# Another order of the same work, and other engines for part of it, in an attention-then-MoE kernel on one core

## The chip, the core and the metric

The kernel runs on one core of a Trainium2 chip. The metric is device time in microseconds from one execution; the median of several executions is given. The engines are TensorE (PE; its weight loads are shown as PEld), VectorE (DVE), ScalarE (ACT), GpSimd (POOL) and SyncE (SP). SP and GpSimd also issue most of the DMAs.

## The reference

```python
scores = scale * np.matmul(q, k.transpose(0, 1, 3, 2))     # q, k, v: 8 x 12 x 448 x 64, fp32
attn = np.maximum(scores, 0.0) ** 2 / S
attn_out = np.matmul(attn, v)
x = attn_out.transpose(0, 2, 1, 3).reshape(B * S, H * D)   # 3584 x 768
h = x @ w_in                                               # 768 x 2048
g = h * (1.0 / (1.0 + np.exp(-1.702 * h)))
out = g @ w_out                                            # 2048 x 768
```

## The kernel before

Attention is cut into 24 units of four heads each (8 batches, 3 units a batch). A unit's q and k are loaded, cast to fp16 and transposed. Then come seven `scores` words s (index j, 64 keys of each head at a time; four 64x64 matmuls of 448 columns into two PSUM banks), relus r out of PSUM to fp16 (one for each bank, on ScalarE or VectorE), one square x on each pair of relus in SBUF, and one `attn_v` word a of 28 matmuls, which needs all seven squares. Copies e bring its result to the token tiles xe and xo.

The token matrix is cut into eight groups g of 384 and 512 tokens in turn. The input product of group 0, and half of group 1, is done by plain matmuls (f, three words for one output tile, each two matmuls). The rest is done by a seven-product scheme in place of eight: sums S of w_in and T of the tokens on VectorE, seven products u of six matmuls, a snapshot t of a bank (ScalarE or VectorE), adds b on VectorE. A gelu g on ScalarE writes fp32 to a `gf` tile, and a widening v takes this to fp16 with a factor. The output product does the same: sums W of w_out and A of the gelus on VectorE, seven products p of eight matmuls for a pair of token tiles (or a single product i), snapshots h, last parts l (all but one kind only on VectorE), and stores o and q.

No scheduler orders this. The body holds one list of 1950 words, and each word issues its instructions when it is reached, under a manual schedule. `f0.2.1` is an f of group 0. `@4.5` names PSUM banks. `:d`, `:a` and `:p` put a word on VectorE, ScalarE or GpSimd, where it has a choice; without it the table `home` decides (`v` on GpSimd, `r`, `t`, `h` and `K` on ScalarE, `Q` on GpSimd) or VectorE takes it. Each engine executes its own instructions strictly in the order in which the words stand. An engine that waits, therefore, holds up all that stands behind it in its queue, DMA issues included. The places of words of different engines relative to each other mean nothing beyond the dependencies.

Loads are words too. On SP's queue: `Lk`, `Lq` load a unit's k or q as fp32 (then `K`, `Q` cast it on an engine, and `Rk`, `Rq` transpose it by DMA), the stores, and one gate `G3`, which waits for a part of w_in. On GpSimd's queue, in this order among its computing: `jk`, `jq` load and cast units 1 to 5, `V` the v of each unit, `jwa` and `jwb` the halves of w_in's four parts, `jo` the four quarters of w_out. Units 0 to 5 are transposed on TensorE (`tk`, `tq`, and copies `ek`, `eq`). `z` words are matmuls of zeros at the start.

The buffers that matter: 11 `at` tiles of squares, 5 `gf`, 3 `osb`, 3 each of `kT` and `qT`, 4 `v16`, one `kst` and one `qst`, and the eight PSUM banks.

```python
        home = {"K": "a", "Q": "p", "r": "a", "t": "a", "h": "a", "v": "p"}
```

```python
    def widen(e, o, i):
        eng[e].tensor_scalar(out=o, in0=i, scalar1=SC, scalar2=1.0, op0=ALU.mult, op1=ALU.mult)
```

In the profile, relus are at lines 161 (VectorE) and 163 (ScalarE), ScalarE's squares at 169, widenings at 217, sums, adds and VectorE's squares at 88, copies at 83, `scores` at 150, `attn_v` at 181, f at 228, all other products at 203, gelus at 214, v, q and k loads of GpSimd at 104, w_in at 411, w_out at 415.

Of the kernel before, what the change touches and what calls it, by code (L numbers as in the profile page):

```python
# [15 lines left out]
def kernel(  # L16
# [406 lines left out]
    with tc.manual_schedule():  # L423
# [35 lines left out]
        def zeros(e, p, n):  # L459
# [8 lines left out]
            "jq1 z13@0 Lk0 I K0:d tk0@1 ek0 z1 Lq0 Q0:a tq0@2 tq1@3 jk1 eq0 s0.1@4.5 jwb2 jk2 "  # L468
            "s0.6@6.7 s0.4@0.1 r0.4.0:d r0.6.0 tk1@2 ek1 jq2 jq3 eq1 s0.3@6.0 r0.1.1 r0.4.1 "
            "r0.1.0 x0.1 s0.0@5.2 r0.0.0 s0.2@1.4 r0.2.0:d r0.3.1:d r0.3.0 s0.5@3.5 r0.6.1 "  # L470
            "s1.1@6.1 r0.2.1 r0.0.1:d s1.2@7.0 s1.5@4.2 x0.0 r0.5.0 r1.1.1 r1.2.1 jk3 x0.4 "
            "r0.5.1:d tq2@3 r1.2.0 x0.2 x0.6:a x0.5 x0.3 V0 r1.5.1 s1.0@1.0 x1.2 tk2@7 r1.5.0:d "
            "r1.0.0 ek2 tk3@5 r1.0.1 jwa0 s1.3@2.1 eq2 r1.1.0 x1.1:a V2 a0@0.6 V1 x1.5:a r1.3.1 "
            "s1.4@4.7 ek3 r1.3.0 jq4 jwb0 s2.1@3.5 r1.4.1 e0.0.1 s2.2@1.2 r1.4.0:d jk4 e0.0.0 "
            "jwa2 s1.6@4.7 x1.3 r1.6.1:d r2.1.0 r2.2.1 tq3@3 r2.2.0 e0.1.0 x1.4 r1.6.0 x1.6 "
            "r2.1.1 x1.0:p s2.6@2.1 jwa1 x2.2 s2.0@7.0 r2.0.1 r2.0.0 a1@4.5 r2.6.1 jwb1 e0.1.1:a "
            "e1.0.0:a s2.5@0.7 s2.3@1.6 r2.3.0 r2.3.1 e1.1.0:a x2.1 eq3 r2.6.0:d e1.0.1:a "
            "s2.4@3.2 r2.5.0:d r2.4.0:d r2.4.1:d jk5 f0.3.0@1 r2.5.1:d f0.2.0@0 x2.0:p tq4@6 eq4 "
            "tk4@4 s3.3@3.2 x2.6:p x2.3:a e1.1.1:a x2.4:p s3.2@7.5 x2.5:a jq5 r3.2.1:d r3.3.1:d "
            "r3.3.0 r3.2.0 f0.3.1 V3 ek4 f0.2.1 f0.0.0@6 s3.0@5.3 a2@2.7 e2.0.0 r3.0.0 S2.1 "  # L480
            "r3.0.1 x3.0:a e2.0.1:a s3.1@4.5 r3.1.0 f0.1.0@3 f0.0.1 f0.1.1 f0.1.2 e2.1.0:a g0.1 "
            "f0.0.2 V4 V5 jwb3 f0.2.2 x3.2 jwa3 g0.0 r3.1.1:d g0.2 f0.3.2 g0.3 x3.3 e2.1.1 "
            "s3.4@4.2 s3.5@5.3 r3.4.1:d s3.6@6.7 f0.8.0@0 f0.8.1 f0.4.0@1 G3 v0.1 r3.5.1:d r3.5.0 "
            "r3.4.0 x3.4 x3.5 x3.1 f0.8.2 f0.4.1 f0.4.2 r3.6.1 g0.8 s4.1@2.5 r3.6.0 v0.3 r4.1.1:d "
            "s4.3@3.4 r4.1.0 s4.2@7.0 r4.2.1 g0.4 f0.6.0@6 f0.6.1 f0.6.2 r4.2.0:d x3.6 tq5@2 "
            "tk5@5 r4.3.0 r4.3.1 x4.3 g0.6 x4.2:a x4.1 ek5 s4.0@0.7 a3@1.3 r4.0.1 r4.0.0 v0.0 "
            "s4.6@4.6 s4.4@7.5 jo0.0 eq5 f0.10.0@0 r4.4.0:d f0.10.1 f0.10.2 x4.0 v0.8 e3.0.0:a "
            "r4.6.1:d r4.4.1 f0.7.0@2 s5.4@1.7 e3.0.1:a s4.5@5.3 r4.6.0 g0.10 s5.1@4.6 v0.10 "
            "r4.5.0 f0.5.0@0 f0.5.1 f0.5.2 x4.6 f0.11.0@5 f0.11.1 f0.11.2 v0.6 f0.7.1 r4.5.1 "
            "r5.4.1 r5.1.0:d r5.1.1:d g0.5 x4.5:a v0.5 f0.7.2 r5.4.0:d s5.0@4.3 x4.4 s5.2@7.6 "  # L490
            "a4@0.1 r5.0.0:d r5.0.1:d g0.7 g0.11 jo0.1 v0.11 s5.6@2.5 r5.2.1 r5.2.0 s5.5@4.6 "
            "s5.3@3.7 r5.6.0:d e4.0.1:a f0.9.0@1 r5.3.1:d r5.3.0 r5.5.1:d v0.7 S0.1 r5.6.1:d "
            "f0.15.0@2 f0.15.1 r5.5.0 f0.14.0@3 x5.6 f1.1.0@7 jo1.1 f0.14.1 x5.5 v0.4 x5.1:a "
            "f0.9.1 v0.2 S3.1 jo1.0 f0.9.2 g0.9 v0.9 f0.13.0@4 f0.13.1 f0.12.0@6 f0.12.1 f1.3.0@5 "
            "e4.0.0:a S2.2 x5.4 Lq6 f0.15.2 Lk6 x5.0:a x5.3:a S2.3 S1.1 x5.2 f1.7.0@1 f0.14.2 "
            "g0.14 f0.12.2 g0.15 g0.12 S3.2 f1.7.1 f0.13.2 f1.5.0@0 Q6:d f1.0.0@3 f1.1.1 S2.4 "
            "g0.13 v0.13 a5@2.6 v0.15 e5.0.0 K6 e5.0.1:a Lk7 v0.14 S1.2 f1.0.1 f1.5.1 T1.1 "
            "f1.4.0@4 T1.2 v0.12 f1.7.2 S3.3 T1.4 W2.1 W0.1 f1.5.2 g1.7 v1.7 f1.6.0@2 A0.0.1@0 "
            "Lq8 g1.5 W3.1 f1.4.1 f1.4.2 g1.4 W2.2 f1.0.2 g1.0 Rk6 Rq6 v1.5 v1.0 f1.6.1 f1.3.1 "
            "u1.2.0@6 f1.2.0@1 t1.2.0 f1.1.2 W1.1 f1.3.2 K7 Rk7 u1.3.0@0 u1.2.1@4 g1.3 g1.1 v1.1 "  # L500
            "v1.3 Q8:a v1.4 f1.6.2 f1.2.1 f1.2.2 g1.2 v1.2 p0.0.0@3 h0.0.0 V8 b1.2.1 t1.3.0:d "
            "u1.3.2 u1.2.2 u1.2.3 Lk8 V6 W2.4 W0.2 T1.3 W2.3 g1.2.1 g1.6 t1.2.2 K8:p s6.0@5.7 "
            "s6.2@1.2 v1.2.1 r6.0.0 W1.2 u1.2.4 W3.2 r6.2.1:d r6.0.1 r6.2.0 t1.2.4 x6.0:a W3.3 "
            "u1.3.1@5 p0.0.1@2 W3.4 b1.3.1 A0.0.2@1 Lq7 s6.1@7.1 u1.2.5 b1.2.3 r6.1.1 r6.1.0:d "
            "l0.0.1 u1.3.3 u1.2.6 s6.3@1.7 W0.4 x6.1:a p0.0.2 W1.3 b1.2.6 Rq8 g1.2.3 r6.3.0:d "
            "t1.3.2 s6.5@4.1 A0.0.4 h0.0.2:d r6.3.1 u1.3.4 W0.3 v1.2.3 p0.0.3 Q7:a v1.6 r6.5.0 "
            "s6.6@7.4 Lq9 Q9 r6.5.1 g1.3.1 g1.2.5 t1.3.4 x6.2:a S3.4 A0.0.3 x6.5:a r6.6.0 W1.4 "
            "v1.3.1 b1.3.3 x6.3 V7 s6.4@1.6 r6.4.0 p0.0.4 u1.3.6 h0.0.4:d u1.3.5 Rq7 r6.6.1 "
            "l0.0.3 r6.4.1:d b1.3.6 p0.0.5 g1.2.6 g1.3.5 s7.4@7.1 s7.0@4.6 g1.3.6 g1.3.3 v1.3.3 "
            "l0.0.5:a v1.3.6 x6.6 s7.2@5.0 r7.2.0 Lk9 x6.4 r7.4.1:d r7.4.0 p0.0.6 r7.2.1 r7.0.0:d "  # L510
            "Rk8 K9:p r7.0.1:d l0.0.6 v1.2.6 x7.0:a s7.1@3.1 r7.1.1 r7.1.0:d a6@5.4 e6.0.0 "
            "e6.0.1:a e6.1.1 Lk11 e6.1.0 s7.5@7.6 s7.3@0.2 r7.5.1:d p1.0.0@3 A0.2.5@1 r7.5.0 x7.1 "
            "r7.3.0 s8.0@1.4 x7.4 s7.6@5.7 r7.6.1:d r8.0.0:d s8.1@0.6 v1.2.5 v1.3.5 r7.3.1 x7.3:a "
            "i0.2.0@2 K11:p r8.1.1 r7.6.0 x7.2 Lq10 x7.5:a x7.6 S1.3 r8.0.1 S0.3 s8.2@6.7 "
            "r8.2.0:d r8.1.0 a7@5.1 s8.3@4.0 o0.1 e7.0.1 Rk9 Rq9 x8.1 r8.3.0:d x8.0 n0.2.0:a "
            "Q10:a r8.2.1 e7.1.1 A1.0.1@0 s8.6@2.6 x8.2:a r8.3.1 i0.2.1@7 r8.6.0 r8.6.1 x8.3:a "
            "h1.0.0 V11 s8.5@0.4 e7.0.0 r8.5.0 x8.6 s8.4@2.1 r8.4.0 r8.4.1 A1.0.2@1 r8.5.1:d "
            "p1.0.1@6 n0.2.1:a x8.4 p1.0.2 e7.1.0:a Lk10 s9.0@0.2 s9.1@1.4 r9.0.0:d r9.1.1:d "
            "l1.0.1 x8.5:a r9.0.1 r9.1.0 a8@7.5 s9.3@2.0 S1.4 x9.0 r9.3.0:d e8.0.0:a K10:p "
            "e8.0.1:a A1.0.4 T2.1 s9.2@1.4 p1.0.3 Rq10 S0.2 r9.2.1 h1.0.2 r9.2.0 r9.3.1 e8.1.0:a "  # L520
            "e8.1.1:a u2.1.0@4 u2.0.0@2 t2.0.0 t2.1.0 u2.0.1@1 s9.4@0.7 u2.1.1@5 Lq11 T2.2 r9.4.0 "
            "b2.0.1 x9.3 u2.1.2 u2.0.2 u2.2.0@0 T2.4 Q11:a b2.1.1 T2.3 g2.0.1 A1.0.3 u2.0.3 "
            "t2.0.2 Rk11 u2.0.4 t2.0.4:d o0.0 g2.1.1 t2.1.2 Rk10 b2.0.3 Lq12 r9.4.1 v2.1.1 u2.1.3 "
            "u2.1.4 Lk12 u2.0.5 t2.2.0 u2.2.1@7 S0.4 v2.0.1 u2.0.6 t2.1.4 x9.1:a b2.1.3 u2.1.6 "
            "b2.2.1 g2.0.3 g2.2.1 u2.2.2 v2.2.1 v2.0.3 b2.0.6 g2.0.6 g2.0.5 v2.0.6 b2.1.6 g2.1.3 "
            "Rq11 u2.1.5 t2.2.2:d v2.1.3 g2.1.5 v2.1.5 u2.2.3 u2.3.0@1 g2.1.6 u2.3.1@5 u2.2.4 "
            "v2.0.5 s9.5@2.4 t2.3.0:d b2.3.1 v2.1.6 u2.3.2 V9 t2.2.4 o0.2 b2.2.3 Q12:a t2.3.2 "
            "A1.2.1@0 A1.2.2@1 g2.3.1 u2.2.5 v2.3.1 u2.3.3 g2.2.3 u2.2.6 r9.5.1 u2.3.4 p1.0.4 "
            "t2.3.4:d u2.3.5 r9.5.0:d b2.2.6 g2.2.5 K12 Lq14 h1.0.4 Lk13 v2.2.3 g2.2.6 g2.3.5 "
            "s10.1@4.0 x9.2 r10.1.1 A1.2.3 x9.4:a l1.0.3 s9.6@2.7 p1.0.5 b2.3.3 s10.0@1.0 u2.3.6 "  # L530
            "v2.2.6 r9.6.0:d r9.6.1 r10.0.0 r10.1.0:d Rk12 V13 b2.3.6 x9.6:a r10.0.1:d Rq12 "
            "p1.2.0@2 g2.3.6 l1.0.5:a x9.5 p1.0.6 l1.0.6 h1.2.0 s10.3@7.4 g2.3.3 s10.2@1.5 Q14 "
            "r10.2.1 r10.2.0 r10.3.0:d a9@0.3 s10.6@6.5 s10.4@7.1 r10.6.0:d x10.0:a r10.6.1:d "
            "p1.2.2 r10.4.1:d e9.0.0:a e9.0.1 x10.1:a v2.3.5 h1.2.2 o1.1 p1.2.1@6 x10.2:a x10.6 "
            "s10.5@0.5 l1.2.1 s11.1@1.3 r10.3.1 r10.5.0:d r10.4.0 x10.4:a x10.3:a r11.1.0:d "
            "p1.2.4 r10.5.1:d r11.1.1:d p1.2.3 s11.0@4.7 s11.3@0.1 v2.2.5 x10.5 h1.2.4 r11.0.0:d "
            "V10 v2.3.6 a10@5.3 r11.3.1 r11.3.0 s11.2@4.1 e10.0.1:a r11.0.1:d l1.2.3 A1.2.4 "
            "v2.3.3 e10.0.0:a Lq13 Q13 K13:p s11.6@7.0 r11.6.0 p1.2.5 x11.1:a o1.0 r11.6.1:d "
            "r11.2.1:d r11.2.0 p1.2.6 A2.0.1@0 s11.5@3.5 s12.3@0.7 x11.0:a s11.4@1.4 l1.2.5:d "
# [135 lines left out]
```

## Time and profile before

| what | value |
|---|---|
| median of 3 runs | 369.36 us (368.82 to 371.6) |
| span of the profiled execution | 372.2 us |
| TensorE busy | 358.6 us, 96% of the span |
| VectorE busy | 302.9 us, 81% |
| ScalarE busy | 281.3 us, 76% |
| GpSimd busy | 137.6 us, 37% |
| granted TensorE clock, mean | 0.987 |
| HBM read, written | 45.61 MB, 11.01 MB |

The profile is of one execution, and its own time is its span, 372.2 us; what lies around the span is not recorded. It is above the slowest of the three timed runs. Busy time counts the union of an engine's instructions. Instructions of one engine overlap by some 0.1 us, so a row's mean duration times its count is more than the engine's busy time. A wait is put down to what ended it.

### The profile page before, as it was taken

What the parts mean: (1) busy time and instruction counts of PE and PEld (TensorE: products, weight loads), DVE (VectorE), ACT (ScalarE), POOL (GpSimd) and SP (SyncE); (2) the same over time, 40 slices, a digit from 0 to 9 for tenths busy, and PEclk for the clock granted to TensorE, in tenths of its full rate; (3) what the DMA queues carried; (4) which work ended last, traced back from release to release, by engine and by line L of the source; (5) the groups of instructions that cost most, each with busy time, mean ns of one, the idle gap of its engine ahead of it and who ended that gap; (6) DMA issues with size and microseconds to landing.
All of it is one profiled execution on the core that took longest, in us unless ns stands there. A gap on an engine that the chain in (4) does not pass through costs nothing.

```text
span 372.2 us, 9025 instructions
## 1 busy us (share of the span) xinstructions
PE 358.6 (96%) x3562; PEld 233.2 (63%) x3562; DVE 302.9 (81%) x556; ACT 281.3 (76%) x540; POOL 137.6 (37%) x202
## 2 busy tenths in 40 slices
PE   7699999799999999999999999999999999999994
PEld 4345554465559755786558755686559755688562
DVE  3988995899988989877998889898897899856552
ACT  3979985579989998798897898868887889346210
POOL 5859264714412732054411613344602421034300
PEclk9989999899999999999999999999999999999998
DMA  9999999918997791849965695784583242300334
GB/s 192 183 204 163 213 209 226 218 18 173 200 225 165 151 221 25 167 105 174 179 170 98 146 184 172 188 171 119 82 205 23 41 97 26 85 2 2 85 97 117
DMA packets 65226, 51.38 MB, mean 138 GB/s; under 512 B 35744, under 2 KB 61856, under 8 KB 65184
## 3 DMA queue, kind: packets, MB, share of 16 engines
q1 hardware_dynamic: 48176, 36.22, 43.2%
q0 software_dynamic: 16608, 14.09, 26.4%
q8 instruction: 28, 0.46, 0.5%
q10 hardware_dynamic: 400, 0.49, 0.4%
q14 instruction: 14, 0.11, 0.1%
HBM read 45.61 MB, written 11.01 MB: 152 GB/s over the span
## 4 chain that ended last, share of the span: by engine, by line
PE 84%; DMA 7%; DVE 3%; POOL 2%; ACT 1%; issue 1%; SPq 0%; DVEq 0%; ACTq 0%
PE ox L203 30%; PE hx L203 27%; PE sc L150 9%; PE av L181 8%; PE os L203 6%; DMA wout<-in_moe_w_out_dram 4%; PE ht L228 3%; DMA v<-in_v_dram 2%; DMA qst<-in_q_dram 1%; DVE wT L88 1%; PE tr L131 1%; POOL ge L217 1%; DVE at L88 1%; ACT gf L214 1%; POOL go L217 0%
## 5 line engine op out<-in xcount | busy, mean ns | idle before, releaser
L163 ACT ACTIVATE at<-sc 128x448 f16<-128x448 f32 x201 | 99.6, 559 | 13.0 <-PE sc L150 12.7
L161 DVE TENSOR_SCALAR at<-sc 128x448 f16<-128x448 f32 x135 | 79.8, 618 | 10.9 <-PE sc L150 10.6
L217 POOL TENSOR_SCALAR go<-gf 128x512 f16<-128x512 f32 x64 | 42.6, 665 | 79.1 <-ACT gf L214 75.7
L169 ACT ACTIVATE at<-at 128x896 f16<-128x896 f16 x72 | 68.2, 962 | 1.7 <-DVE at L161 1.2
L217 POOL TENSOR_SCALAR ge<-gf 128x384 f16<-128x384 f32 x64 | 35.4, 554 | 74.0 <-ACT gf L214 70.8
L203 PEld LDWEIGHTS <-win 128*128 128x128 f16 x624 | 56.7, 98 | 8.5 <-issue 2.4
L88 DVE TENSOR_TENSOR at<-at 128x896 f16<-128x896 f16 x92 | 55.9, 631 | 1.7 <-ACT at L163 0.6
L88 DVE TENSOR_TENSOR gf<-hx,gf 128x512 f32<-128x512 f32 (+1 forms) x78 | 47.7, 625 | 11.5 <-ACT gf L79 5.4
L150 PE MATMUL sc<-qT,kT 64*64 64x448 f16 x672 | 52.6, 363 | 1.3 <-DVE qT L83 0.6
L214 ACT ACTIVATE gf<-gf 128x512 f32<-128x512 f32 (+1 forms) x78 | 43.8, 585 | 11.7 <-DVE gf L88 11.6
L203 PEld LDWEIGHTS <-winS 128*128 128x128 f16 x468 | 43.4, 99 | 8.2 <-issue 3.9
L203 PE MATMUL ox<-wout,go 128*128 128x384 f16 x256 | 46.4, 326 | 0.0
L203 PEld LDWEIGHTS <-go 128*128 128x128 f16 x320 | 29.9, 98 | 23.2 <-issue 5.8
L203 PE MATMUL hx<-T,winS 128*128 128x256 f16 (+1 forms) x312 | 38.2, 268 | 2.7 <-DVE gf L83 2.7
L181 PE MATMUL av<-at,v 64*64 64x448 f16 x672 | 37.5, 357 | 1.0 <-DMA v<-in_v_dram 1.0
L203 PEld LDWEIGHTS <-ge 128*128 128x128 f16 x256 | 24.0, 98 | 18.4 <-issue 4.1
L150 PEld LDWEIGHTS <-kT 64*64 64x64 f16 x672 | 18.7, 106 | 26.3 <-issue 22.1
L79 ACT ACTIVATE gf<-hx 128x384 f32<-128x384 f32 (+1 forms) x44 | 23.3, 537 | 15.4 <-PE hx L203 12.0
L203 PE MATMUL ox<-wT,asum 128*128 128x384 f16 x192 | 34.9, 327 | 0.0
L203 PE MATMUL hx<-xo,win 128*128 128x256 f16 x252 | 31.4, 273 | 0.4 <-ACT gf L79 0.4
L203 PEld LDWEIGHTS <-asum 128*128 128x128 f16 x224 | 21.1, 98 | 16.3 <-issue 3.3
L81 ACT ACTIVATE osb<-ox 128x384 f32<-128x384 f32 x32 | 15.4, 496 | 19.2 <-PE ox L203 19.1
(75 smaller groups left out, 475.9 us busy)
## 6 DMA issues: line engine op xcount, KB each, us to landing
out_dram<-osb SPq DMA_DIRECT2D x52, 192.0 KB, 3.2
kst<-in_k_dram SPq DMA_DIRECT2D x19, 448.0 KB, 4.7
qst<-in_q_dram SPq DMA_DIRECT2D x19, 448.0 KB, 4.9
v<-in_v_dram POOLq DMA_DIRECT2D x24, 224.0 KB, 5.6
win<-in_moe_w_in_dram POOLq DMA_DIRECT2D x8, 384.0 KB, 9.7
wout<-in_moe_w_out_dram POOLq DMA_DIRECT2D x4, 768.0 KB, 11.5
q<-in_q_dram POOLq DMA_DIRECT2D x5, 224.0 KB, 5.6
k<-in_k_dram POOLq DMA_DIRECT2D x5, 224.0 KB, 6.5
```

Of the source, the lines that this page charges most:

```text
L79: nc.scalar.activation(out=o, in_=i, func=AF.Copy)
L81: nc.scalar.activation(out=o, in_=i, func=AF.Copy, scale=scale)
L88: eng[e].tensor_tensor(out=o, in0=x, in1=y, op=op)
L150: nc.tensor.matmul(out=sc[a][c, 0:S], lhsT=st["kT"][r, j, c], rhs=st["qT"][r, :, c], start=True, stop=True)
L161: nc.vector.tensor_scalar(out=o, in0=i, scalar1=0.0, scalar2=None, op0=ALU.max)
L163: nc.scalar.activation(out=o, in_=i, func=AF.Relu)
L169: nc.scalar.activation(out=at, in_=at, func=AF.Square)
L181: nc.tensor.matmul(out=av[s][64 * a:64 * a + 64, 0:S], lhsT=v16[r, a, 64 * j:64 * j + 64], rhs=at[r, a, :], start=(j == 0), stop=(j == J - 1))
L203: nc.tensor.matmul(out=o, lhsT=lhs(i), rhs=rhs(i), start=start and i == 0, stop=i == n - 1, skip_group_check=True)
L214: nc.scalar.activation(out=o, in_=i, func=AF.Gelu_apprx_sigmoid, scale=1.0 / SC)
L217: eng[e].tensor_scalar(out=o, in0=i, scalar1=SC, scalar2=1.0, op0=ALU.mult, op1=ALU.mult)
L228: nc.tensor.matmul(out=hp[g, f][:, 0:n], lhsT=w[:, i, fo:fo + 128], rhs=xts[g][:, i, 0:n], start=i == 0, stop=i == NK - 1)
```

## The change

Only the list of words is replaced. Both lists hold the same 1950 operations; none is left out or added. Their order differs on every engine, and so do the PSUM banks named, and the engines of these (VectorE / ScalarE / GpSimd, before and after; a dash where there is none):

| words | before | after |
|---|---|---|
| relus r | 135 / 201 / - | 108 / 228 / - |
| squares x | 92 / 72 / 4 | 96 / 72 / - |
| widenings v | - / - / 128 | 33 / - / 95 |
| snapshots t | 34 / 44 / - | 28 / 50 / - |
| snapshots h | 12 / 24 / - | 17 / 19 / - |
| last parts l | 40 / 8 / - | 48 / - / - |
| copies e | 32 / 40 / - | 34 / 38 / - |
| casts K and Q | 4 / 16 / 18 | 7 / 7 / 24 |
| copies eq | 6 / - / - | 5 / 1 / - |
| last stores q, on SP / ScalarE | 3 / 5 | 4 / 4 |

The start, the loads of w_out and the first sums W of it, and the end of the list, as the diff has them:

```diff
-            "jq1 z13@0 Lk0 I K0:d tk0@1 ek0 z1 Lq0 Q0:a tq0@2 tq1@3 jk1 eq0 s0.1@4.5 jwb2 jk2 "
...
-            "s4.6@4.6 s4.4@7.5 jo0.0 eq5 f0.10.0@0 r4.4.0:d f0.10.1 f0.10.2 x4.0 v0.8 e3.0.0:a "
...
-            "a4@0.1 r5.0.0:d r5.0.1:d g0.7 g0.11 jo0.1 v0.11 s5.6@2.5 r5.2.1 r5.2.0 s5.5@4.6 "
...
-            "f0.15.0@2 f0.15.1 r5.5.0 f0.14.0@3 x5.6 f1.1.0@7 jo1.1 f0.14.1 x5.5 v0.4 x5.1:a "
-            "f0.9.1 v0.2 S3.1 jo1.0 f0.9.2 g0.9 v0.9 f0.13.0@4 f0.13.1 f0.12.0@6 f0.12.1 f1.3.0@5 "
...
-            "f1.4.0@4 T1.2 v0.12 f1.7.2 S3.3 T1.4 W2.1 W0.1 f1.5.2 g1.7 v1.7 f1.6.0@2 A0.0.1@0 "
...
-            "q7.2.0.0 p7.0.6 h7.2.4 l7.2.3 q7.3.1.0:a q7.2.0.1:a l7.0.6 o7.0 p7.2.5 l7.2.5:d "
-            "q7.3.0.0:a q7.3.0.1 q7.3.1.1:a p7.2.6 l7.2.6 q7.2.1.0:a q7.2.1.1"
+            "jq1 z13@0 z1 jk1 I jwb2 Lq0 Q0:a tq0@1 Lk0 jq2 K0:d tk0@2 eq0 ek0 jk2 tq1@3 eq1 "
...
+            "r2.2.0 r2.1.1 V5 x2.0 e1.0.0:a eq3 e1.1.0 s2.6@3.1 e1.0.1:a x2.1 jo1.0 r2.6.0 e1.1.1 "
+            "s2.3@5.7 s2.5@6.2 r2.3.0 r2.3.1:d x2.2 r2.5.1 jo0.0 f0.3.0@4 f0.3.1 r2.6.1:d s3.3@3.0 "
+            "s3.2@5.7 r3.2.1:d r3.3.1 r3.3.0 tk4@2 r2.5.0:d tq4@1 x2.3:a ek4 jo1.1 r3.2.0 x2.4 "
...
+            "r3.1.0 e2.1.1:a e2.0.0 jo0.1 r3.1.1:d x3.1 f0.1.0@1 f0.1.1 f0.1.2 x3.2 f0.3.2 r3.0.0 "
+            "f0.2.2 g0.1 g0.3 v0.3:d f0.0.0@5 v0.1:d g0.2 s3.5@2.6 s3.6@3.0 r3.6.0 s3.4@1.4 r3.6.1 "
...
+            "A0.0.1@0 u1.2.1@0 b1.2.1 W0.1 f1.0.1 f1.3.0@5 f1.3.1 f1.3.2 W2.1 A0.0.3 f1.2.0@2 S3.3 "
...
+            "q7.3.1.1:a p7.2.6 l7.2.5 q7.3.0.1:a q7.3.1.0 q7.3.0.0 q7.2.0.0 l7.2.6 q7.2.1.1:a "
+            "q7.2.1.0"
```

On GpSimd's queue the order of the loads becomes jq1 jk1 jwb2 jq2 jk2 V0 jk3 V1 jq3 jwb0 jwa0 jk4 jq4 V2 jwa2 jwb1 jwa1 jk5 jq5 V3 jwb3 jwa3 V4 V5 jo1.0 jo0.0 jo1.1 jo0.1, all of them ahead of its first widening (v0.2). Before, it was jq1 jk1 jwb2 jk2 jq2 jq3 jk3 V0 jwa0 V2 V1 jq4 jwb0 jk4 jwa2 jwa1 jwb1 jk5 jq5 V3 V4 V5 jwb3 jwa3, with the four squares among them, and then jo0.0, jo0.1, jo1.1 and jo1.0 among the widenings of group 0. W.1 needs jo1.0 and jo0.0, W.2 and W.3 jo1.1, W.4 jo0.1.

## The prediction

> **What bounds the kernel now.** I read the page first, then the waits, the chain of waits, the stretches and the timeline, and last the two word lists against them.
>
> ```profile
> PE 358.6 (96%) x3562; PEld 233.2 (63%) x3562; DVE 302.9 (81%) x556; ACT 281.3 (76%) x540; POOL 137.6 (37%) x202
> ...
> PEclk9989999899999999999999999999999999999998
> ```
>
> TensorE is busy nearly everywhere, but busy is not peak. So I priced its words at the pace that they have back to back: an output product (p) 1.30 us ("ox x16" takes 2.60 in the chain), an input product (u) 0.655 with 512 columns and 0.495 with 384, an `attn_v` (a) 1.32, a pair of `f` matmuls 0.326 or 0.433, a `scores` word (s) 0.19. 84 p (109.2) + 8 i (20.8) + 182 u (105.8) + 72 f (26.1) + 24 a (31.7) + 168 s (31.8) + transposes and zero matmuls (9.2) = 334.6 us. The span is 372.2, so 37.6 are lost, and the timeline says where: the last matmul ends at 367.4 (4.8 of tail); `a2` starts at 30.3 with 17.2 us of TensorE words behind it (13.1 lost by then, 14.9 by `a5` at 57.3); `s6.0` starts at 75.9 behind 56.3 (19.6 lost); from there to the end 13 more.
>
> ```profile
> PE hx L203 <- DVE gf L83: 2.7, 1, 2.7
> PE tr L131 <- DVE at L88: 1.2, 1, 1.2
> ...
> PE av L181 <- DMA v<-in_v_dram: 1.0, 1, 1.0
> ```
>
> TensorE's waits: the largest is on a snapshot on VectorE. The chain leads it back further.
>
> ```profile
> 51.51 14.72 DMA wout<-in_moe_w_out_dram
> 67.27 0.63 DVE asum L88
> 68.29 2.72 DVE wT L88 x3
> 71.01 0.60 DVE gf L88
> 71.61 0.61 DVE gf L83
> 72.26 3.75 PE hx L203 x18
> ```
>
> The snapshot stood in VectorE's queue behind the sums W of w_out, and these waited (3.85 us of idle VectorE before 66.32) for the last quarter of w_out.
>
> ```profile
> core 0: us, PE busy (x) PEld busy (x) DVE busy (x) ACT busy (x) POOL busy (x), PEclk, DMA share, GB/s
> 17.00:21.00 4.00, 3.30 (x40) 1.74 (x41) 2.14 (x5) 2.34 (x5) 3.35 (x4) 0.62 1.24 195
> 21.00:72.00 51.00, 47.93 (x496) 26.35 (x489) 43.13 (x77) 41.06 (x84) 29.81 (x39) 1.00 1.18 206
> 72.00:76.00 4.00, 3.74 (x22) 2.47 (x25) 4.00 (x7) 1.36 (x3) 2.26 (x3) 0.57 1.01 164
> 76.00:366.00 290.00, 289.59 (x2850) 195.30 (x2850) 242.01 (x448) 225.50 (x430) 90.67 (x137) 1.00 0.59 121
> ```
>
> After that stall the clock is halved (0.57): three u words take 0.98, 1.28 and 1.42 us. The stall costs 2.9 + 1.7 = 4.6 us. In the first 72 us the DMA engines are full (1.18). From 76 to 366 TensorE hardly idles.
>
> ```profile
> 44.13 1.28 POOL L217 TENSOR_SCALAR ge<-gf 128x384 f16<-128x384 f32 x2 [5.88 <-ACT gf L214]
> 45.91 0.51 POOL L217 TENSOR_SCALAR ge<-gf 128x384 f16<-128x384 f32 x1 [0.50 <-ACT gf L214]
> 46.48 0.92 POOL L415 DMA_DIRECT2D wout<-in_moe_w_out_dram  x1
> 47.93 1.09 POOL L217 TENSOR_SCALAR ge<-gf 128x384 f16<-128x384 f32 x2 [0.53 <-ACT gf L214]
> 49.08 0.91 POOL L415 DMA_DIRECT2D wout<-in_moe_w_out_dram  x1
> 50.06 1.39 POOL L217 TENSOR_SCALAR ge<-gf 128x384 f16<-128x384 f32 x2
> 51.51 0.92 POOL L415 DMA_DIRECT2D wout<-in_moe_w_out_dram  x1
> ```
>
> This is why w_out is late: GpSimd issues it between widenings that wait for ScalarE's gelus.
>
> [...] W sums take 0.96 beside widenings (68.3 to 71.0) and 0.55 without. [...] Here VectorE's 896-wide fp32 cast takes 614 ns, where a 512-wide copy from PSUM takes 687; no widening on VectorE is in this trace.
>
> **The change part by part.** No matmul goes or comes: 334.6 stays. The diff gives the counts; the cost of one is its distance to the next when back to back (ScalarE relu 0.44, VectorE relu 0.54, squares 0.855 and 0.54; the rows' means overlap).
>
> 1. Engines. VectorE: 27 relus leave (-14.5), 4 squares (+2.2), 8 last parts (+3.8), 5 output snapshots (+2.6) and casts and evacuations (+2.0) come, 6 snapshots go (-3.6), and 33 widenings come: 16 of 512, 17 of 384. From the 614 ns cast [...] I estimate 0.33 and 0.26, +9.7 in all; the upper end is a PSUM copy's pace, 0.64 and 0.52, +19. Sum +2.2, at most +12. ScalarE +1.5 (27 relus +11.9; casts, snapshots and last parts leave). GpSimd -24: 4 squares (-7.0), 33 widenings (-22.8), 6 casts more (+5.9).
>
> 2. w_out. The four loads now stand ahead of every widening on GpSimd's queue. They wait for nothing but their place: 16 q, k, v units of 224 KB, 8 w_in halves of 384 KB, then 4 of 768 KB, 9.97 MB, at the 195 GB/s of the full stretch, is 51 us; from 5 us on, and with 2.5 us for unit 6's loads on SP's queue, the last lands near 59 (66.2 before), the first two, which W.1 needs, near 50. The first W stands behind 46.5 us of TensorE words, near 60. The wait goes, and with it the half clock. What is late next is VectorE: between `a5` and `a6` its sum is 32.2 us (29.1 before) against 29.3 of TensorE words (30.5 with their switches). The stage took 35.1. VectorE enters it ahead of the plan (6.3 us of work in the 8.6 between `a4` and `a5`) and can do w_in's sums early; I take 31.8. Gain 3.3; with widenings at the upper end (5 fall here, 0.3 more each) 1.8; if VectorE never matters 4.6.
>
> 3. Start. The first q goes ahead of k on SP, unit 1's k leaves GpSimd at about 2.2 (2.7 before), V0 stands sixth instead of eighth on GpSimd's queue and lands near 14 (17.65), so `a0` no longer waits for it. But `a0` also needs all squares of unit 0: VectorE has 10.9 us of work before it in both orders, ScalarE 9.6, from about 5.5 us with some 0.7 idle, so `a0` starts near 17.0 (17.7). From there to `a5` took 39.6; TensorE 33.0 in both, VectorE 33.7 to 32.5, ScalarE 33.7 to 35.8, GpSimd's four squares (1.8 each) gone. I leave 39.6. Gain 0.7, between -1 and 2.5.
>
> 4. From `a6` on. TensorE loses 0.11 us each time that it changes between 64x64 scores and 128x128 products (mean of the 99 changes after 80 us in the timeline). The new order has 43 + 44 such changes after unit 6 begins, the old 51 + 51: -1.6 us. Against it: ScalarE and VectorE stages that slightly exceed TensorE's (`a9` to `a10` VectorE 8.9 in a stage that took 8.1; `a13` to `a14` ScalarE 7.4 in 6.6). 11 `at`, 5 `gf` and 3 `osb` buffers cover most of it; 0.8 if not. Net gain 0.8, between -2 and 1.5.
>
> 5. Loads later on. SP's casts, transposes and stores are all reordered. I counted each unit's distance in TensorE words from the last thing that holds its transpose to its first scores. The shortest is 6.3 us (k of unit 21), where before has 3.4 to 5.3 without a stall and a transpose takes 3 to 8 from issue to landing. Of the v loads on GpSimd, V18 stands behind v5.1.6 and has 9.9 us, of which the gelu chain takes about 4 (the median from product to widening) and the load 4 to 6.5. Cost nothing, up to 1.5 for `a18`.
>
> 6. Tail. Last product, last sum and a half store follow as before; 4.8 stays, within 0.4.
>
> Sum: -3.3 - 0.7 - 0.8 = -4.8 us: 372.2 to 367.4 for the profiled execution. Its span is above the median of the runs, 369.36 (368.82 to 371.6), so the stall may be smaller in them. I take the same 4.8 off the median: 364.6.
>
> **Rivals.**
> A: the w_out stall is mostly the profiled execution's. For: its span lies 2.8 above the median, and the runs spread by as much. Against: GpSimd's order makes w_out late in any run. Then the gain is 0.7 + 0.8 and a third of 3.3: 2.6, 366.8; with dear widenings 368.
> B: slower. VectorE executes in order, and each of its 33 widenings now waits there for a gelu, with snapshots and adds that free TensorE's banks behind it. Before shows the price: adds waited 5.4 us in 9 cases for ScalarE's snapshots, 0.6 each. It loses once more than 8 of the waits fall where VectorE is the bound (4.8 / 0.6); with 16 of them, 9.6 - 4.8 = +4.8: 374.2. Against: from `a11` on TensorE has 209 us of words and VectorE 172, so most waits there are free.
> C: more gain. V0's early landing also removes the first half clock (1.7), and nothing new waits (0.7 more): 362.2.
>
> **How the numbers follow.** Forecast 0.58, A 0.22, B 0.10, C 0.10. The forecast's own range is 362.3 to 366.9. C and A extend it to 361.0 and 368.5, which leaves out B and little else. This kernel's measurement tells about 1%, 3.7 us. Faster by over 1% (below 365.7): three quarters of the forecast, C and a little of A, 0.57; within 1%: 0.33; slower: B, 0.10.
>
> **What would show it.** Right: no VectorE wait on w_out; the only halved clock near 17 to 21; `a6` near 88 (92.5 before); VectorE's widenings at about 410 and 350 ns; TensorE's busy share up and its words 334.6 again; GpSimd busy near 115. Wrong: a TensorE wait of over 1 us after 76, a halved clock in mid-kernel, VectorE waiting many times for gelus with adds late behind them, widenings of 650 ns, or `a5` later than 58.

## The result, and the profile after

The changed kernel takes 366.46 us in the median of 4 runs (365.47 to 367.25), the kernel before 369.09 on the same chip (368.7 to 371.6). The measured ratio is 0.9881 (0.9832 to 0.9929), so it is faster by 1.2%. The quotient of these two medians of four is 0.993; that of all runs made here (366.47 in 10 of after, 370.95 in 139 of before) is 0.988. The changed kernel's profiled execution took 365.47 us with a span of 363.7, which is 8.5 less than the first profile of before. The medians differ by 2.6 only, so much of the 8.5 belongs to that one execution of before. In all that follows, medians are of all runs of a kernel, and a ratio leaves out runs of more than 1.5% above the kernel's fastest.

The page of the profile after, in the lines that were shown of before (busy time and its share of the span, and the granted TensorE clock in 40 slices):

```profile
PE 355.3 (98%) x3562; PEld 231.8 (64%) x3562; DVE 309.6 (85%) x577; ACT 283.2 (78%) x550; POOL 123.4 (34%) x171
...
PEclk9999999999999999999999999999999999999999
```

The same stretches as before: length, busy time of each engine, granted clock, DMA share, GB/s.

```profile
17.00:21.00 4.00, 3.78 (x57) 1.76 (x55) 4.00 (x10) 4.00 (x11) 3.16 (x6) 1.00 1.24 205
21.00:72.00 51.00, 50.14 (x507) 28.26 (x505) 46.17 (x88) 43.70 (x88) 25.07 (x32) 1.00 1.20 214
72.00:76.00 4.00, 4.00 (x38) 2.85 (x35) 3.83 (x8) 3.55 (x7) 0.79 (x1) 1.00 1.05 102
```

Both halved clocks are gone (0.62 and 0.57 before), and TensorE is busy throughout the third stretch. Its longest waits are that of the first zero matmul and two more:

```profile
PE zp L463 <- DVE wT L456: 1.2, 1, 1.2
PE sc L150 <- ACT at L163: 0.7, 1, 0.7
PE ht L228 <- DVE xe L83: 0.3, 1, 0.3
```

The new rows, VectorE's widenings (busy us, mean ns of one, and idle time before them):

```profile
L217 DVE TENSOR_SCALAR go<-gf 128x512 f16<-128x512 f32 x16 | 6.6, 419 | 3.3 <-ACT gf L214 3.3
L217 DVE TENSOR_SCALAR ge<-gf 128x384 f16<-128x384 f32 x17 | 5.9, 358 | 1.0 <-ACT gf L214 0.9
```

Where did the time go? I use the prediction's own measure: the time at which a word starts, less the prices of all TensorE words ahead of it. That is the time lost so far. "Before 2" and "after 2" are second profiles of the same two kernels, from the experiments.

| lost, us | before | before 2 | after | after 2 |
|---|---|---|---|---|
| up to `a2` | 13.1 | 12.3 | 10.7 | 11.3 |
| `a2` to `a5` | 1.8 | 1.8 | 2.3 | 2.3 |
| `a5` to `a6` | 6.1 | 3.5 | 1.4 | 1.4 |
| `a6` to the last matmul | 11.9 | 12.1 | 10.6 | 11.6 |
| tail behind it | 4.8 | 4.7 | 4.1 | 4.1 |
| span | 372.2 | 369.0 | 363.7 | 365.3 |

The stage between `a5` and `a6` gives most: 4.7 of 8.5 between the first profiles, 2.1 of 3.7 between the second ones. The start gives 1.0 to 2.4, of which 0.5 goes again before `a5`. The rest of the order gives 0.5 to 1.3, and the tail 0.6.

### The profile page after: what moved, and what is told of

Read it like the earlier page. It is cut to its first block, busy times and chain, and to the rows that moved or that the text cites. A ratio compares the mean times of both kernels' runs of the same rounds, so it can differ in the third digit from the quotient of the medians.

```text
span 363.7 us, 9020 instructions
## 1 busy us (share of the span) xinstructions
PE 355.3 (98%) x3562; PEld 231.8 (64%) x3562; DVE 309.6 (85%) x577; ACT 283.2 (78%) x550; POOL 123.4 (34%) x171
## 4 chain that ended last, share of the span: by engine, by line
PE 87%; ACT 5%; DVE 5%; DMA 1%; issue 1%; SPq 0%; ACTq 0%
PE ox L203 29%; PE hx L203 29%; PE sc L150 9%; PE av L181 8%; PE ht L228 7%; PE os L203 4%; ACT at L163 3%; DVE at L161 1%; DMA kst<-in_k_dram 1%; ACT at L169 1%; DVE at L88 1%; ACT xe L79 1%; DVE asum L88 1%; PE tr L131 1%; DVE xe L83 0%
## 5 line engine op out<-in xcount | busy, mean ns | idle before, releaser
L163 ACT ACTIVATE at<-sc 128x448 f16<-128x448 f32 x228 | 111.5, 574 | 13.6 <-PE sc L150 12.2
L161 DVE TENSOR_SCALAR at<-sc 128x448 f16<-128x448 f32 x108 | 64.4, 615 | 5.1 <-PE sc L150 4.6
L88 DVE TENSOR_TENSOR at<-at 128x896 f16<-128x896 f16 x96 | 61.4, 657 | 3.2 <-ACT at L163 2.7
L217 POOL TENSOR_SCALAR go<-gf 128x512 f16<-128x512 f32 x48 | 35.9, 747 | 71.2 <-ACT gf L214 57.5
L150 PE MATMUL sc<-qT,kT 64*64 64x448 f16 x672 | 51.7, 359 | 1.7 <-ACT at L163 0.7
L217 POOL TENSOR_SCALAR ge<-gf 128x384 f16<-128x384 f32 x47 | 29.4, 626 | 65.7 <-ACT gf L214 63.7
L203 PEld LDWEIGHTS <-winS 128*128 128x128 f16 x468 | 42.5, 98 | 5.5 <-issue 1.6
L203 PE MATMUL hx<-T,winS 128*128 128x256 f16 (+1 forms) x312 | 36.8, 260 | 0.0
L79 ACT ACTIVATE gf<-hx 128x512 f32<-128x512 f32 (+1 forms) x50 | 26.3, 542 | 11.0 <-PE hx L203 7.6
L181 PEld LDWEIGHTS <-v 64*64 64x64 f16 x672 | 20.5, 107 | 11.9 <-issue 2.1
## 6 DMA issues: line engine op xcount, KB each, us to landing
win<-in_moe_w_in_dram POOLq DMA_DIRECT2D x8, 384.0 KB, 10.7
wout<-in_moe_w_out_dram POOLq DMA_DIRECT2D x4, 768.0 KB, 22.3
```

The costliest lines, as they stand in the source:

```text
L79: nc.scalar.activation(out=o, in_=i, func=AF.Copy)
L88: eng[e].tensor_tensor(out=o, in0=x, in1=y, op=op)
L150: nc.tensor.matmul(out=sc[a][c, 0:S], lhsT=st["kT"][r, j, c], rhs=st["qT"][r, :, c], start=True, stop=True)
L161: nc.vector.tensor_scalar(out=o, in0=i, scalar1=0.0, scalar2=None, op0=ALU.max)
L163: nc.scalar.activation(out=o, in_=i, func=AF.Relu)
L181: nc.tensor.matmul(out=av[s][64 * a:64 * a + 64, 0:S], lhsT=v16[r, a, 64 * j:64 * j + 64], rhs=at[r, a, :], start=(j == 0), stop=(j == J - 1))
```

## The experiments

All are timed beside runs of before. Each group of four ran on a chip of its own, so a comparison across groups also carries the difference of two chips; before's three medians lie within 1.2 us. These four were measured together (before: 370.81 us in 47 runs).

**1. Before once more.** No edit.

> The kernel before once more, unchanged, to see how much of the first profile belongs to that one execution. Theory 1 (the stall on w_out is in every run): span of 370 us or more in its profile, VectorE idle for 3 to 4 us before the first W, and a halved TensorE clock behind it. Theory 2 (rival A: it is mostly the first profile's): span of 366.8 to 368.0, VectorE's wait for w_out under 1.5 us, TensorE's wait for the snapshot behind it under 1 us, and a mean clock of 0.993 or more, with at most one stretch at half clock (the one near 18 to 21 us).

Measured: 371.77 us (368.32 to 376.26, 14 runs), ratio to itself 1.0015 (0.9972 to 1.0058). The profiled execution had a span of 369.0 at a clock of 0.999. The stretches:

```profile
17.00:21.00 4.00, 2.51 (x48) 1.30 (x44) 3.27 (x7) 3.63 (x7) 3.63 (x4) 1.00 1.25 202
...
72.00:76.00 4.00, 2.80 (x23) 1.63 (x21) 4.00 (x8) 2.12 (x5) 0.83 (x2) 1.00 0.71 116
```

And VectorE's wait there, from its waits between 55 and 80 us:

```profile
DVE wT L88 <- DMA wout<-in_moe_w_out_dram: 2.3, 1, 2.3
```

Neither theory holds alone. VectorE's wait is there (2.3 us, 3.9 in the first profile), but no clock is halved behind it. The kernel before varies: over the 139 runs of it in these comparisons the median is 370.95, and they reach from 367.99 to 376.48. The times go with the mean clock: 369.0 in the 45 runs at 0.9965 or more, 370.9 in the 50 between that and 0.9925, 373.0 in the 44 below. The 10 runs of the changed kernel, at 0.995 to 1.0, lie between 365.22 and 367.25. TensorE's pauses don't tell the two profiles apart: in the first, TensorE pauses for 1.24 and 0.95 us between 14.6 and 17.7, and the clock is halved (0.50) from 17.9 to 21.4; in the second it pauses for 0.77, 0.86 and 0.86 us between 13.2 and 18.0, no less in all, and the clock stays full (1.00).

**2. Before, w_out first.**

```diff
-  jwa3 g0.0 ... (jo0.0, jo0.1, jo1.1, jo1.0 among the widenings)
+  jwa3 jo1.0 jo0.0 jo1.1 jo0.1 g0.0 ...
```

> The kernel before with one part of the change: the four loads of w_out directly behind the last load of w_in on GpSimd's queue, ahead of all widenings, in the order of the changed kernel; nothing else is moved. Theory 1: 4.0 to 4.6 us less than before (ratio 0.988). Theory 2: 0.5 to 1.5 us less (ratio 0.996 to 0.999). A third reading (the loads then collide with unit 3 to 6's q, k, v on the DMA engines): slower by 0.5 us or more, with a TensorE wait before a3 or a4. In all of them no VectorE wait on w_out is left.

Measured: 369.88 us (368.71 to 371.74, 14 runs), ratio 0.998 (0.9947 to 1.0014). `a5` to `a6` loses 1.9 instead of 3.5. The lowest run is no lower than before's (368.7 beside 368.2), but none is above 372, where before reaches 375: this would fit a stall whose cost differs between executions, as it does between the two profiles of before (6.1 and 3.5 lost there).

**3. After, w_out late.**

```diff
-  ... x2.1 jo1.0 r2.6.0 ... jo0.0 ... jo1.1 ... jo0.1 r3.1.1:d ...
+  ... v0.10 jo1.0 ... v0.15 jo0.0 ... v0.8 jo1.1 ... v0.7 jo0.1 ...
```

> The changed kernel with its four loads of w_out put back among the widenings of group 0 on GpSimd's queue (behind v0.10, v0.15, v0.8 and v0.7). Theory 1: the stall comes back, with a VectorE wait of 3 us or more and a halved clock behind it: 4 us more than the changed kernel, 370.5. Theory 2: 0.5 to 1.5 us more, 367 to 368. If nothing changes, w_out's place on the queue is worth nothing and the gain lies in the rest of the order.

Measured: 366.82 us (365.35 to 368.22, 10 runs), and 1.5 us lost between `a5` and `a6`. Nothing happened, although the loads were issued at 43.6 to 53.3 us instead of 31.5 to 35.6. So their place behind the widenings, to which the prediction put the stall, isn't enough to make it. I had overlooked something else: the order of the four. The first sums W.1 need jo1.0 and jo0.0. Before issues jo1.0 last, and experiments 2 and 3 both issue it first.

**4. After, all widenings on GpSimd.** Edit: `:d` is taken off the 33 v words.

> The changed kernel with all 33 widenings of VectorE back on GpSimd, at the same places of the order. VectorE loses 12 us of busy time (419 and 358 ns each), GpSimd gains some 20. My step 1 (engines off TensorE's path): within 0.7 us of the changed kernel, 366 to 367. Rival B (the widenings in VectorE's queue delay adds and snapshots): 1.5 us or more faster than the changed kernel. A third reading (GpSimd's longer, later widenings hold up the output products or slow VectorE's fp16 sums): 1.5 us or more slower, with TensorE waits for widenings, and sums W and T at over 0.6 us each.

Measured: 368.21 us (366.79 to 369.79, 22 runs), 1.6 more than the changed kernel's 366.62 (experiment 7, on another chip), and 1.4 more than experiment 3 on the same chip. Three places lose 0.6 to 0.9 each. The chain of waits shows the first:

```profile
38.16 7.71 DMA kst<-in_k_dram
...
46.00 0.93 POOL k L83
46.93 0.08 issue
47.01 0.77 POOL ge L217
47.78 0.08 issue
47.86 0.52 POOL ge L217
48.38 0.02 issue
48.40 0.49 ACT gf L214
```

Two widenings stand behind a cast of unit 6's k on GpSimd, and the cast waits for its load. The widenings hold `gf` tiles, so a gelu on ScalarE waits for one, and behind it `scores`, a copy to xo on ScalarE and TensorE's next f words wait. In the changed kernel the same two ran on VectorE at 41.9 and 42.2 us. The third reading was right on the size, through another mechanism than the two it named.

The next four together (before: 369.98 us in 51 runs).

**5. After's first 220 words, then before's order.**

> A splice: the first 220 words are those of the changed kernel (its start, up to shortly before a3, with w_out's loads first and two widenings on VectorE), and all remaining words stand in the order and on the engines of before. It has 12.3 us lost by a2 in before's second profile and 10.9 in the changed kernel's. Theory S (the start's gain survives to the end): w_out first gave 369.9, less 1.4 to 2.2 for the start, 367.7 to 368.5 (ratio about 0.993). Theory L (the later order makes the gain, the start's time is taken up by the next wait): no better than w_out first alone, 369.5 to 370.

Measured: 370.41 us (369.42 to 371.78, 14 runs), ratio 1.0008 (0.9978 to 1.0039). Of the start's gain (11.4 lost by `a2`; 10.7 and 11.3 in the two profiles of after) 1.6 goes again between `a2` and `a5`, where this splice loses 3.4 us, and the tail is 5.5 in it. In this splice the start is worth nothing in the runs. That it pays together with the words behind it is an inference. Its profile also has a clock halved from 14.4 to 17.8 (mean clock of the execution 0.991), which neither profile of the changed kernel has (0.999 and 1.0).

**6. Before's first 499 words, then after's order.**

> The reverse splice: the first 499 words are those of before (about 80 us, to p0.0.5), and all remaining words stand in the order and on the engines of the changed kernel. Between unit 6 and the last attn_v TensorE lost 13.4 us in before's second profile and 11.4 in the changed kernel's, mostly in changes between 64x64 and 128x128 matmuls (98 against 83). Theory L: 1.5 to 2 us less than before, 368.8 to 369.3 beside its 370.8, with 11 to 11.5 us lost after 80 us. Theory S (only the start and w_out gain): within 0.5 us of before.

Measured: 369.26 us (366.79 to 371.34, 22 runs), ratio 0.9948 (0.9919 to 0.9977). Its profile loses 10.9 from `a6` on and 4.4 in the tail; its lowest run is 1.6 below before's (366.8 beside 368.4), the ratio is worth 1.9 us, the medians differ by 0.7. Theory L holds in the ratio; the stall of the first 76 us is still there (3.6 lost between `a5` and `a6` in its profile).

**7. After once more.** No edit.

> The changed kernel once more, unchanged, so that it stands beside the others on one chip, with more runs. 366.4 to 366.8 us and a clock of 0.995 to 1.0 in nearly every run; its runs spread by less than 3 us, where before's spread by 8. If its runs spread as far as before's, the narrower spread of the first runs was chance, and the gain is not in the stalls of the first 76 us.

Measured: 366.62 us (365.22 to 367.16, 6 runs), ratio 0.9884 (0.9835 to 0.9934). The first comparison repeats, and so does the narrow spread.

**8. Before, V0 two places up.**

```diff
-  ... jk2 ... jq2 jq3 ... jk3 ... x0.3 V0 ...
+  ... jk2 ... jq2 V0 jq3 ... jk3 ... x0.3 ...
```

> The kernel before with one word moved: the load V0 two places up on GpSimd's queue, ahead of jq3 and jk3 (sixth instead of eighth, as in the changed kernel). In both profiles of before a0 waits 0.9 us for V0. If V0 is what holds a0 back: the wait goes, and in the runs in which it led to a halved clock that goes too; 0.9 to 1.7 us less, 369.1 to 369.9. If a0 is held by the squares of unit 0 all the same (my step 3: near 17.0 us): the wait passes to VectorE or ScalarE and 0.3 us or less is gained. A third way: k and q of unit 3 come later, tq3 or tk3 waits, and the loss cancels the gain.

Measured: 372.76 us (369.04 to 376.85, 22 runs), ratio 1.0047 (1.0016 to 1.0077): slower. TensorE's waits up to 60 us begin with

```profile
PE tr L131 <- DMA k<-in_k_dram: 2.8, 1, 2.8
```

V0 landed at 14.6 instead of 17.9 and unit 3's k at 17.2 instead of 16.2, and tk3 stands ahead of `a0`. This is the third way. In the changed kernel tk3 stands behind `a0`, which may be why an early V0 doesn't hurt there; that was not tried alone.

The last four together (before: 371.17 us in 27 runs).

**9. Before, the four loads in after's order, places kept.**

```diff
-  ... v0.0 ... jo0.0 ... v0.5 ... jo0.1 ... v0.7 ... jo1.1 ... v0.2 S3.1 jo1.0
+  ... v0.0 ... jo1.0 ... v0.5 ... jo0.0 ... v0.7 ... jo1.1 ... v0.2 S3.1 jo0.1
```

> The kernel before with the four loads of w_out in the same four places among the widenings, but in the changed kernel's order: jo1.0, jo0.0, jo1.1, jo0.1 instead of jo0.0, jo0.1, jo1.1, jo1.0. The first sums W.1 need jo1.0 and jo0.0 alone, and before issues jo1.0 last. Theory O (the order of the four is what counts): no VectorE wait on w_out, and a result like that of w_out first, 369.5 to 370 us with no run above 372.5. Theory P (their place behind the widenings counts): the wait stays at 1.5 to 4 us, and the runs reach 374 to 376 as in before.

Measured: 369.13 us (367.95 to 371.65, 22 runs), ratio 0.9965 (0.9938 to 0.9991); 2.0 us less in the median. No wait on w_out is left, and `a5` to `a6` loses 1.9, as in experiment 2.

**10. After, w_out late and in before's order.** As experiment 3, with jo0.0, jo0.1, jo1.1, jo1.0 in the four places.

> The changed kernel with the loads of w_out late, among the widenings as in the run before with late loads, and now in the order of before, jo1.0 last. Theory O: the stall comes back, a VectorE wait of 2 to 5 us before the first W, and 2 to 4 us more than the changed kernel's 366.6, 368.6 to 370.6. Theory P or neither: 366.5 to 367.2, as with the late loads in the new order.

Measured: 375.65 us (374.14 to 377.13, 6 runs), ratio 1.015 (1.0096 to 1.0204). VectorE's waits:

```profile
DVE wT L88 <- DMA wout<-in_moe_w_out_dram: 9.4, 1, 9.4
```

And the stretches from 62 us, with columns as above:

```profile
62.00:70.00 8.00, 6.91 (x40) 3.65 (x38) 0.00 (x0) 2.84 (x5) 2.47 (x4) 1.00 1.25 222
70.00:72.00 2.00, 0.00 (x0) 0.00 (x0) 1.32 (x3) 0.00 (x0) 0.00 (x0) 1.00 0.88 139
72.00:80.00 8.00, 4.12 (x22) 3.09 (x23) 6.93 (x16) 4.41 (x8) 0.00 (x0) 0.57 0.21 59
```

This is the cleanest pair of the study. Experiments 3 and 10 issue four loads at the same times to 0.01 us (43.6, 48.3, 50.6, 53.3), and the last lands at 70.6 in both. Only which quarter stands in which place differs. That is worth 8.8 us between the medians, which come from two chips, and 9.0 in the stage from `a5` to `a6` of the two profiles (39.7 and 30.7). VectorE stands still from 62 to 70, the snapshots and gelus behind it too, and TensorE runs dry at 68.9.

**11. After, four squares back on GpSimd.** Edit: `:p` on x1.0, x2.0, x2.4 and x2.6.

> The changed kernel with the four squares that before has on GpSimd (x1.0, x2.0, x2.4, x2.6) there again. They took 1.8 us each on GpSimd and about 0.55 on VectorE. If they cost nothing off TensorE's path (my step 1): within 0.5 us of the changed kernel, 366.1 to 367.1. If they hold up the loads behind them on GpSimd's queue (k and q of unit 5, V3 to V5, the last of w_in and w_out) or the attn_v that needs them: a1 and a2 up to 1.5 us later, 367.3 to 368.5.

Measured: 377.67 us (376.79 to 379.31, 6 runs), ratio 1.0204 (1.015 to 1.0259). Both theories were far too low. GpSimd's timeline (start, length, what, idle time before it and its releaser):

```profile
26.00 0.66 POOL L411 DMA_DIRECT2D win<-in_moe_w_in_dram  x1 [0.43 <-DMA v<-in_v_dram]
28.22 0.71 POOL L104 DMA_DIRECT2D v<-in_v_dram  x1 [1.56 <-DMA win<-in_moe_w_in_dram]
30.11 0.70 POOL L104 DMA_DIRECT2D v<-in_v_dram  x1 [1.19 <-DMA win<-in_moe_w_in_dram]
30.84 1.69 POOL L88 TENSOR_TENSOR at<-at 128x896 f16<-128x896 f16 x1
32.46 2.69 POOL L415 DMA_DIRECT2D wout<-in_moe_w_out_dram  x3
35.15 3.34 POOL L88 TENSOR_TENSOR at<-at 128x896 f16<-128x896 f16 x2
```

The squares of unit 2 stand behind load issues, and these issues wait themselves until earlier loads have landed. `a2`, which starts at 27.5 in the changed kernel, gets its last square at 38.5 us, and the clock falls to a mean of 0.70 between 28 and 45. This isn't the place that the squares have in before (there they stand ahead of jq5 and all of V3 to V5); it shows that the changed order, with its loads first, loses 11 us with these squares on GpSimd.

**12. After, two words moved.**

```diff
-  A1.0.1@0 r8.2.1:d i0.2.1@0 r8.3.1 A1.0.3 r8.3.0 Rk11 A1.0.2@1 ...
+  A1.0.1@0 r8.2.1:d i0.2.1@0 r8.3.1 r8.3.0 Rk11 A1.0.2@1 ... S0.4 A1.0.3 ...
...
-  s13.1@6.3 ... r13.0.1 ... u3.3.6 s13.3@4.5
+  u3.3.6 s13.1@6.3 ... s13.3@4.5
```

> The changed kernel with two words moved. In two of three of its profiles p1.0.2 waited 1.1 us near 100 us for the sum A1.0.2, which stands behind A1.0.3 on VectorE while GpSimd casts beside it; A1.0.3 is needed 15 us later. It is moved behind S0.4. And u3.3.6 is moved ahead of s13.1, which saves two changes between 64x64 and 128x128 matmuls at 0.1 us each. Expected: no wait of p1.0.2, 0.6 to 1.3 us less than the changed kernel, 365.3 to 366.0. If the wait only passes to the squares of unit 8 (a8): 0.2 us or less.

What it is aimed at is seen on VectorE in the second profile of after, and its counterpart on GpSimd:

```profile
97.00 0.68 DVE L88 TENSOR_TENSOR asum<-go 128x1024 f16<-128x1024 f16 x1
97.60 0.62 DVE L161 TENSOR_SCALAR at<-sc 128x448 f16<-128x448 f32 x1
98.13 1.42 DVE L88 TENSOR_TENSOR go<-go 128x1024 f16<-128x1024 f16 x1
99.48 1.75 DVE L88 TENSOR_TENSOR asum<-asum,go 128x1024 f16<-128x1024 f16 x1
```

```profile
98.08 0.93 POOL L83 CAST k<-kst 128x896 f16<-128x896 f32 x1 [2.60 <-DMA kst<-in_k_dram]
...
99.74 0.94 POOL L83 CAST q<-qst 128x896 f16<-128x896 f32 x1
```

A sum of 0.68 takes 1.42 and 1.75 beside GpSimd's casts, and p1.0.2 waited 1.1 us for it. Measured: 366.03 us (365.37 to 366.77, 6 runs), 0.6 below the changed kernel's 366.62; the ratios to before (0.9886 and 0.9884) don't separate them. The wait of p1.0.2 is gone in the profile: its lead over after's second profile grows there from 0.5 to 1.7 us. The move of u3.3.6 lost 0.6 again in place of gaining 0.2, as `a12` then waited 0.4 on VectorE. At the last matmul 1.35 are left. But after's first profile doesn't have the wait either (the same sum took 0.68 us there), and its last matmul ends 0.25 us before that of this experiment. It is the best median of the study, and that the two moves earned it is not shown.

## Why the prediction was right, and where it wasn't

The sum, -4.8, holds better than the predicted time. Taken from the median of 370.95 that before has in 139 runs, it gives 366.15, beside 366.47 in 10 runs of after. It was taken from the median of three runs, 369.36, which was 1.6 too low; that is most of the distance between 364.6 and 366.46. That -4.8 fits so well is in part luck. Its largest term, 3.3, is the difference of 35.1, the stage `a5` to `a6` of an execution with a large stall, and 31.8, which was 1.2 too much for the stage after (30.6). Before's second profile takes 32.5 there, from which the same step would have had 0.7.

Step 1, the engines. My estimates of VectorE's widenings, 410 and 350 ns, started from the 614 ns cast, but no trace of before shows how its time goes with the width; measured were 419 and 358. The total of VectorE rose by 6.7, not 2.2: its squares took 657 ns instead of 631, so that their row grew by 5.5 where 2.2 was put, and the widenings' 12.5 was put at 9.7. GpSimd fell by 14.2, not 24: its widenings took 747 and 626 ns instead of 665 and 554. None of these amounts entered the predicted sum: step 1 was put at nothing for TensorE, and that failed. Experiment 4 prices the widenings' move at 1.6 us and experiment 11 the squares' at 11 in this order, both through what stands behind a wait on GpSimd.

Step 2, w_out: right in the stage and near in size (3.3 predicted; 4.7 between the first profiles, 2.1 between the second), with half of the cause. "GpSimd issues it between widenings that wait for ScalarE's gelus" is true (5.88 us at the longest in both profiles of before), but it makes no wait as long as jo1.0 goes first (experiments 3 and 9). Late loads together with the old order, in which the quarter that the first sums need is issued last, do make one (experiment 10). Early loads in the old order were not run. Judged by the landings, they would leave no wait in before, where the last quarter lands at 61.2 and the first W starts at 62.3 in experiment 2; in the changed kernel some 3.4 us of wait would be left, as its last quarter lands at 64.4 and its first W starts at 61.0. These are estimates from the traces.

The landing was mis-sized as well: the last quarter landed at 64.4, not near 59.

```profile
L415 POOL DMA_DIRECT2D wout<-in_moe_w_out_dram x4: 873/874/881, 31.5 to 35.6; - x4
...
DMA to landing us min/median/max: 15.8/22.3/28.7
```

The four loads were issued from 31.5 to 35.6 us and took 22.3 us to land in the median, 11.5 before: what was issued early waited on DMA engines that are full either way (1.20 and 1.18). Issued 16 us earlier than before, the last landed 1.9 us earlier; issued 17.6 us earlier than in experiment 3, it landed 6.2 us earlier. The term of the landing that failed is the one for SP's queue, 2.5 us: up to 64.4 us its loads and transposes moved 3.1 MB, some 15 us at the 209 GB/s of that time, beside the 10.2 MB of GpSimd's. It didn't matter, because the first two quarters landed at 47.3 and 51.8, and the sums of the later ones come at 68.5. The next bound, VectorE between `a5` and `a6`, did not show: 30.6 us passed, where 31.8 were put.

Step 3, the start: `a0` came at 15.4 (17.0 predicted), `a5` at 55.2 (56.6). The gain of 0.7 was 1.9 between the first profiles at `a5`, 0.5 between the second (the table). Over more profiles, `a0` comes at 16.6 to 18.4 with before's start (before, experiments 1, 2, 6 and 9) and at 15.3 to 16.0 with after's (after, 3, 4, 5, 7, 10 and 12). So the bound by squares, 17.0, was too late; what sets `a0` in the new order was not taken apart. That the first half clock would stay was wrong for all profiles of the changed order, but experiment 5, with the same first 220 words, has it. Experiment 8 shows that the credit doesn't go to V0's place alone.

Step 4, from `a6` on: right. 0.8 was predicted; 1.3 and 0.5 were measured, and experiment 6 gives 0.7 in the medians and 1.9 by its ratio. After 80 us, a change from a 128x128 to a 64x64 word cost 0.092 us in the median, one back 0.103, and a word behind one of its kind 0.00; there were 83 changes, 98 in before's second profile. Of the new stalls, the one near 100 us (experiment 12) was the largest; it is in after's second profile and not in its first.

Step 5: no TensorE wait on a load after 76 us, as said. Step 6: the tail is 4.1, not 4.8. In before's second profile, the last store's issue on ScalarE stands behind another issue there and starts 0.22 us after the last sum; in the first of after it starts 0.03 after it. The rest, some 0.4 us, is left for the landing.

The rivals. A was half right: the stall was larger in the first profile than in the second (6.1 and 3.5), but the second has it too. How often the runs at the lower clock have it isn't shown. Its 366.8 lies nearer to 366.46 than the forecast, with the low base. B: VectorE waited 4.2 us for gelus in its 33 widenings (the two rows above), and TensorE waited for no add. C's half clock went from the profiles, but its reason, V0, doesn't do that alone: experiment 8 has it from 17.7 to 21.1 (0.59 in the mean of 17 to 21).

What is left open: by the ratios, the order of the four loads is worth 1.3 us in before (experiment 9) and the words from 499 on 1.9 (experiment 6), of 4.3 in all. The rest, some 1 us, would be the start and the words up to there; no experiment isolates it, and experiment 5 didn't find it.

## What to carry to other kernels

When a load is late, look first at which of its parts the first reader needs: on DMA engines as full as here (1.20) an earlier issue moved the last landing by about a third of its lead at most (6.2 of 17.6 us), while the order decided which part came last. On a queue that executes in order, price an instruction by what stands ahead of it and what it holds (a buffer, a square, a bank), not by its duration: in experiment 11, four squares of 1.7 to 1.8 us each cost 11 us. Take one profile as one draw: compare two of the same kernel before a stall is given a price, and several runs before a base is subtracted from.

## What was not expected of the hardware

- The order of four loads, issued at equal times, was worth 8.8 us in the changed kernel (experiments 3 and 10).
- GpSimd's load issues can wait for earlier loads to land, 1.19 and 1.56 us at a time in experiment 11, by the releasers that the profile infers. What limits them wasn't tried.
- VectorE's sums of 128x1024 fp16 took 1.42 and 1.75 us beside GpSimd's casts, and 0.68 just ahead of them (second profile of after, 97.0 to 101.2). It reached TensorE: p1.0.2 waited 1.1 us behind these sums. Why they slow down is not shown.
- Whether a pause of TensorE near the start halves the clock differed between executions. The first profile of after and that of experiment 5 have the same first 220 words and the same longest pause there (0.70 us, from 13.0 and 12.9 us on); the clock was halved in experiment 5 alone, from 14.4 to 17.8. In the first profile of before the clock is halved for 3.41 us each time up to the last matmul, and the full stretches behind these two, 51.20 and 293.55 us, are 15 and 86 times that.
